# Order of the start, banks of the output weights, a second junk buffer and shuffled priorities in an attention-then-SoLU kernel

## The chip, the cores and the metric

The kernel runs on one core of a Trainium2 chip. The metric is device time in microseconds (us) of one execution. The engines are PE (TensorE), ACT (ScalarE), DVE (VectorE), POOL (GpSimd) and SP (SyncE, which issues nearly all DMAs); each takes its own instructions strictly in the order in which the program lists them, and waits on semaphores for the others.

## The reference

Two layers run one after the other. The first is attention over a set with 32 inducing points: per batch (4 batches of 12608 rows of 128 channels) `h = mab(inducing, x)` pools all rows into 32 vectors, and `mab(x, h)` lets every row attend to these 32. The second is a feed-forward layer of width 1024 on each of the 50432 rows:

```python
def mab(q, kv):
    s = scale * (q @ kv.transpose(0, 2, 1))
    s = s - s.max(-1, keepdims=True)
    a = np.exp(s)
    a /= a.sum(-1, keepdims=True) + 1e-09
    return a @ kv
h = mab(I, x); y = mab(x, h)              # 4 x 12608 x 128
h = y @ w_in                              # 128 -> 1024
e = np.exp(h - h.max(-1)); solu = h * e / (e.sum(-1) + 1e-09)
mu = solu.mean(-1); var = ((solu - mu) ** 2).mean(-1)
out = ((solu - mu) / np.sqrt(var + 1e-06) * g_ln) @ w_out    # 1024 -> 128
```

Attention inputs are 32-bit floats; the three weights of the second layer come as 64-bit floats and are rounded on the chip.

## The kernel before, in words

A tile is 128 rows of x; a batch has 99 tiles, the whole job 396. Four tiles make a group.

*Phase 1 of a batch* (`p1`) reads x, transposes it on PE, copies it out on ACT, stores the transposed x in DRAM, takes scores against the inducing points, a running maximum (DVE, with a small matmul that folds the four row groups), the exponentials (ACT), a transposition (DVE), and a weighted sum on PE. `combine` turns the sum into h and multiplies it by the input weights (`h4`, `hs`). Batch 0 runs this at the start of the kernel, in nine pieces of up to 12 tiles; the phase 1 of a later batch runs in between the tiles of the batch ahead.

*Phase 2 of a batch* (`p2`) computes each row's 32 attention weights, transposed (`aT`).

*The body* goes over the tiles. PE multiplies `aT` by `hs` (L1233, two matmuls of 512 columns, which use two of the four 32-row groups of the array); DVE scales and takes the row minimum (L1275); ACT takes the exponential and its sum (L1286); POOL multiplies (L1290); ACT squares the product for the variance (L1301), of which only the accumulated sum is used: the squares themselves go to a junk buffer `sq`; DVE transposes the product into `vt` (L1317). When four tiles of a group have come, PE multiplies them by the output weights `wc` in 32 steps of small matmuls (L1473), for each pair of row groups; these fill the row groups that L1233 leaves free. `evacuate` (L1501, DVE or ACT) and `finish` (L1526 to L1551) normalize and store.

*The weights.* `weights_in` and `weights_out` load and round the 64-bit weights (L434 to L454, on DVE, ACT and POOL). The output weights are then scaled by the gains (L492, ACT, eight instructions), their mean is taken (L501, PE) and subtracted (L506, DVE), and each quarter is spread to all four row groups (L544, PE; L522, copies by ACT or DVE) into `wc`.

*Memory for results of PE.* At the start the PSUM is cut into eight banks of 512 columns (`bank_e`, the locks `EARLY_TR` and `EARLY_PB`); `handover` gives it up for four buffers of 1024 (`h0` to `h3`, the lock `H`) that the body uses. The handover waits for phase 1 of batch 0, for `hs`, for the first `aT`, and for `wc`.

*What sets the order.* Each job is a generator that yields operations with a planned cost and a priority. The class `Planner` keeps a clock for each engine; among the operations of an engine that would be ready within a slack (`SLACK`) it takes the one with the lowest priority number, and writes its instruction. So the order on every engine is fixed when the program is built, from planned costs. A tile's priority number is its place t in the job; an offset for each kind of operation is added to it. PE's idle time is filled with transposes of the identity (L557), which do no work.

The function `beats` writes steps of PE: in each it emits one matmul for each of the two pairs of row groups that has work.

Of the kernel before, what the change touches and what calls it, by code (L numbers as in the profile page):

```python
# [10 lines left out]
BF16 = mybir.dt.bfloat16  # L11
# [8 lines left out]
P = 128  # L20
# [20 lines left out]
SLOTS = 3  # L41
PIECE = 4
TOKENS = 4
TURN_ON = 90
# [23 lines left out]
FILL = 400  # L68
FIRST = 4
LATE = -15  # L70
# [20 lines left out]
WOUT_X = -16.5  # L91
WOUT = -8
WIN = -18.5
# [22 lines left out]
class Op:  # L116
    def __init__(self, eng, cost, fn, *after, prio=None, alt=None, moves=0, late=0):
        self.eng, self.cost, self.fn, self.after, self.prio, self.alt, self.moves = eng, cost, fn, after, prio, alt, moves
        self.late = late
# [22 lines left out]
class Planner:  # L142
# [61 lines left out]
    def _pe(self, start, cost):  # L204

        at = start
        while True:
# [8 lines left out]
            self.busy[k] = self.busy.get(k, 0.0) + took  # L216
# [20 lines left out]
    def run(self):  # L237
        clock = self.clock
        while self.ops:
            first = min(self.ops, key=lambda o: (max(clock[o[0].eng], o[1]), o[3]))  # L240
            eng = first[0].eng
            limit = max(clock[eng], first[1]) + self.slack[eng]
            pick = min(
                (o for o in self.ops if o[0].eng == eng and o[1] <= limit),
                key=lambda o: (o[2][1] if o[0].prio is None else o[0].prio, o[3]),
# [8 lines left out]
            end = start + (self._pe(start, op.cost) if eng == "PE" else op.cost)  # L254
# [9 lines left out]
def set_attention_then_solu_kernel(ctx: ExitStack, tc: tile.TileContext, x, inducing, w_in, w_out, g_ln, out):  # L264
# [55 lines left out]
    sq = buf([P, FF], "sq", BF16)  # L320
# [14 lines left out]
    BULK = Lock([None] * TOKENS)  # L335
    ST = Lock([
# [84 lines left out]
    w_in_ready = Event()  # L421
# [54 lines left out]
    def weights_in():  # L476
        g = yield from rounded(w_in_sb, w_in.bitcast(U32), conv, None, conv_free, WIN)
# [5 lines left out]
    def weights_out():  # L483
# [12 lines left out]
        yield turned[NP[0] - 1]  # L496
        mp, rel = yield EARLY_PB.at(LATE)

# [4 lines left out]
        d = yield Op("PE", KC * 215, mean, d, rel, prio=LATE)  # L503
# [7 lines left out]
        give(EARLY_PB, mp, d)  # L511
# [7 lines left out]
        last, laid = [], [o]  # L519
# [4 lines left out]
        def laid_out(sp, q, k0, dp):  # L524
            dc = yield Op(
                "ACT", 570, out_of(nc.scalar.copy, sp, q, k0), dp, o, prio=LATE,
                alt=Op("DVE", 620, out_of(nc.vector.tensor_copy, sp, q, k0), dp, o, prio=LATE),
            )
            give(EARLY_PB, sp, dc)
# [4 lines left out]
        def spread(k0):  # L534
            four, free = [], []
            for q in range(4):
                sp, rel = yield EARLY_PB.at(LATE)
                four.append(sp)
                free += rel

            def copies():
                for q, sp in enumerate(four):
                    r = slice(q * M, (q + 1) * M)
                    nc.tensor.matmul(sp, lhsT=fold2[r, :], rhs=wg2[r, k0 * C : (k0 + half) * C], start=True, stop=True)  # L544

            dp = yield Op("PE", 1200, copies, d, free, prio=LATE)
            last.append(dp)
            if len(last) == 2:
                give(HN, wg2, *last)
            for q, sp in enumerate(four):  # L550
                spawn(laid_out(sp, q, k0, dp), LATE)

        for k0 in (0, half):
            spawn(spread(k0), LATE)
# [43 lines left out]
    def p1(b, k):  # L598
# [9 lines left out]
        halves = [(0, GS), (GS, n)] if early and not k and n > GS else [(0, n)]  # L608
        if not early:
            halves = [(c, min(c + PIECE, n)) for c in range(0, n, PIECE)]  # L610
        for c0, c1 in halves:
            for nbytes, fn in move(b, s0 + c0, c1 - c0, xn[:, c0:, :], False):
                trel = () if early else (yield BULK)[1]
                d = yield dma(nbytes, fn, rel, trel)
                if not early:
                    give(BULK, None, d)
# [1063 lines left out]
```

## Time and profile before

| what | value |
|---|---|
| time, median of 3 runs | 1184.61 us (1183.17 to 1184.68) |
| the profiled execution's own time | 1182.92 us |
| its span, first to last instruction | 1181.1 us |
| PE, busy | 1151.1 us, 97% |
| ACT, busy | 1102.6 us, 93% |
| DVE, busy | 1074.8 us, 91% |
| POOL, busy | 1065.6 us, 90% |
| tiles | 396 |

The profile is of one execution. The ends of matmuls are modelled, so that PE's 97% is not PE at its peak. An engine's idle time counts only what lies between its records; two records of one engine can overlap where one instruction's end runs beside the next one's start.

### The profile page before, as it was taken

What the parts mean: (1) busy time and instruction counts of PE and PEld (TensorE: products, weight loads), DVE (VectorE), ACT (ScalarE), POOL (GpSimd) and SP (SyncE); (2) the same over time, 40 slices, a digit from 0 to 9 for tenths busy, and PEclk for the clock granted to TensorE, in tenths of its full rate; (3) what the DMA queues carried; (4) which work ended last, traced back from release to release, by engine and by line L of the source; (5) the groups of instructions that cost most, each with busy time, mean ns of one, the idle gap of its engine ahead of it and who ended that gap; (6) DMA issues with size and microseconds to landing.
All of it is one profiled execution on the core that took longest, in us unless ns stands there. A gap on an engine that the chain in (4) does not pass through costs nothing.

```text
span 1181.1 us, 68196 instructions
## 1 busy us (share of the span) xinstructions
PE 1151.1 (97%) x30636; PEld 1055.0 (89%) x30636; DVE 1074.8 (91%) x1639; ACT 1102.6 (93%) x2191; POOL 1065.6 (90%) x612
## 2 busy tenths in 40 slices
PE   9999999999999999999999999999999999999996
PEld 7669989998889898999899999999988999999996
DVE  6799989898999899999899998999999999999981
ACT  5699899999999999999999999999999999999994
POOL 3399799898999989899899998989999999999994
PEclk9989999999999999999999999999999999999999
DMA  9532342522143433331423433341313131220103
GB/s 340 230 124 76 111 121 71 155 73 49 41 119 86 141 111 107 96 104 33 120 66 94 121 107 120 102 127 45 101 40 84 40 79 34 67 64 5 49 5 87
DMA packets 166884, 110.62 MB, mean 94 GB/s; under 512 B 78112, under 2 KB 131776, under 8 KB 166464
## 3 DMA queue, kind: packets, MB, share of 16 engines
q1 hardware_dynamic: 166592, 106.27, 31.0%
q8 instruction: 239, 3.92, 1.4%
q14 instruction: 53, 0.43, 0.1%
HBM read 53.51 MB, written 52.17 MB: 89 GB/s over the span
## 4 chain that ended last, share of the span: by engine, by line
PE 45%; POOL 23%; ACT 20%; issue 7%; DVE 3%; DMA 2%; SPq 0%; ACTq 0%; POOLq 0%; DVEq 0%
PE h L1473 32%; POOL eu L1290 16%; ACT sq L1301 9%; ACT eu L1286 6%; PE h L1233 4%; POOL spare L1290 3%; POOL spare L1547 3%; ACT spare L1286 1%; ACT xT L666 1%; ACT spare L1501 1%; PE h L850 1%; PE h L655 1%; ACT a L1013 1%; PE bank_e L557 1%; DMA dl<-dd 1%
## 5 line engine op out<-in xcount | busy, mean ns | idle before, releaser
L1473 PEld LDWEIGHTS h<-wc,vt 32*128 32x128 f32 (+1 forms) x25344 | 954.3, 185 | 45.8 <-issue 13.3
L1473 PE MATMUL h<-wc,vt 32*128 32x129 f32 (+1 forms) x25344 | 983.5, 273 | 10.4 <-ACT spare L1501 3.1
L1290 POOL TENSOR_TENSOR eu<-hn,eu 128x1024 f32<-128x1024 f32 x198 | 466.8, 2377 | 28.7 <-ACT eu L1286 27.7
L1233 PE MATMUL h<-hs,aT 32*128 32x512 f32 x1584 | 419.6, 607 | 6.0 <-DVE spare L1275 2.6
L1317 DVE STREAM_TRANSPOSE vt<-eu 128x1024 f32<-128x1024 f32 x327 | 397.7, 1229 | 11.4 <-POOL eu L1290 10.7
L1301 ACT ACTIVATE sq<-eu 128x1024 bf16<-128x1024 f32 x330 | 346.4, 1050 | 11.3 <-POOL eu L1290 6.5
L1290 POOL TENSOR_TENSOR eu<-spare,eu 128x1024 f32<-128x1024 f32 x132 | 311.7, 2379 | 11.2 <-ACT eu L1286 11.1
L1275 DVE TENSOR_SCALAR_CACHE_REDUCE hn<-h,rn 128x1024 f32<-128x1024 f32 x198 | 248.7, 1260 | 20.6 <-PE h L1233 12.2
L1275 DVE TENSOR_SCALAR_CACHE_REDUCE spare<-h,rn 128x1024 f32<-128x1024 f32 x198 | 248.2, 1260 | 20.7 <-PE h L1233 10.0
L1286 ACT ACTIVATE eu<-hn,nm 128x1024 f32<-128x1024 f32 x198 | 225.4, 1139 | 2.9 <-DVE hn L1275 2.7
L1290 POOL TENSOR_TENSOR spare<-spare 128x1024 f32<-128x1024 f32 x66 | 156.9, 2377 | 12.2 <-ACT spare L1286 12.2
L1286 ACT ACTIVATE eu<-spare,nm 128x1024 f32<-128x1024 f32 x132 | 150.4, 1140 | 2.3 <-DVE vt L1317 1.3
L1233 PEld LDWEIGHTS h<-hs,aT 32*128 32x128 f32 x1584 | 124.6, 186 | 27.5 <-DVE spare L1275 8.1
L1317 DVE STREAM_TRANSPOSE vt<-spare 128x1024 f32<-128x1024 f32 x65 | 80.0, 1231 | 2.0 <-POOL spare L1290 1.8
L1547 POOL TENSOR_TENSOR spare<-spare,fin 128x512 f32<-128x512 f32 x79 | 79.8, 1041 | 1.6
L1301 ACT ACTIVATE sq<-spare 128x1024 bf16<-128x1024 f32 x66 | 69.3, 1050 | 6.9 <-POOL spare L1290 5.3
L1286 ACT ACTIVATE spare<-spare,nm 128x1024 f32<-128x1024 f32 x66 | 75.2, 1140 | 0.4 <-DVE spare L1275 0.4
L1301 ACT ACTIVATION_READ_ACCUMULATOR sq<-eu 128x1 f32 x330 | 62.6, 190 | 0.0
L655 PE MATMUL h<-ident,xn 32*128 32x32 f32 x1188 | 53.6, 227 | 0.1
L655 PEld LDWEIGHTS h<-ident,xn 32*128 32x128 f32 x1188 | 51.1, 141 | 1.1 <-issue 0.8
L1501 ACT COPY spare<-h 128x774 f32<-128x774 f32 (+3 forms) x66 | 42.5, 646 | 9.3 <-PE h L1473 7.0
L666 ACT COPY xT<-h 128x1024 f32<-128x1024 f32 (+2 forms) x42 | 37.8, 900 | 1.1 <-PE h L655 1.1
(189 smaller groups left out, 849.6 us busy)
## 6 DMA issues: line engine op xcount, KB each, us to landing
out_dram<-spare SPq DMA_DIRECT2D x95, 256.0 KB, 3.3
xT<-xd SPq DMA_DIRECT2D x93, 256.0 KB, 3.8
xn<-in_x_dram SPq DMA_DIRECT2D x73, 256.0 KB, 3.7
xd<-xT SPq DMA_DIRECT2D x72, 256.0 KB, 2.6
dl<-dd SPq DMA_DIRECT2D x392, 1.0 KB, 2.3
xd<-vt SPq DMA_DIRECT2D x7, 768.0 KB, 10.2
spare<-in_x_dram SPq DMA_DIRECT2D x5, 768.0 KB, 9.3
dd<-qe SPq DMA_DIRECT2D x95, 4.0 KB, 2.1
```

The lines of the kernel that those rows point to most:

```text
L557: nc.tensor.transpose(out=bank[:, :P], in_=ident, identity=ident)
L655: nc.tensor.transpose(out=tr[:, k * 512 + s * M : k * 512 + (s + 1) * M], in_=xn[r, s, :], identity=ident[r, r])
L666: lambda: nc.scalar.copy(xT.rearrange("c s (q t) -> c q s t", q=4)[:, 2 * w : 2 * w + 2, :n, :], tr.rearrange("c (k x) -> c k x", k=2)[:, ...
L1233: nc.tensor.matmul(hp[:, cols], lhsT=aT[rows, i // 2, :], rhs=hs[rows, cols], start=True, stop=True)
L1275: lambda: nc.vector.tensor_scalar(out=hn, in0=hp, scalar1=rn, scalar2=None, op0=ALU.mult, op1=ALU.min, accum_out=nm),
L1286: "ACT", 1133, lambda: nc.scalar.activation(e, hn, AF.Exp, bias=nm, scale=-1.0, accum_out=G["qe"][:, s, 1:2]), d, rel, srel,
L1290: d = yield Op("POOL", 2330, lambda: nc.gpsimd.tensor_tensor(out=e, in0=hn, in1=e, op=ALU.mult), de, prio=t + PR_MU)
L1301: "ACT", 1040, lambda: nc.scalar.activation(sq, e, AF.Square, scale=1.0 / 32.0, accum_out=G["qe"][:, s, 0:1]), d,
L1317: lambda: nc.vector.transpose(out=G["vtb"][:, : n * FF].rearrange("p (j s t) -> p j s t", j=M, s=n)[:, :, s, :], in_=e.rearrange("p (a f) ...
L1473: nc.tensor.matmul(op[:rows, a - 2 * w, :], lhsT=vt[q, k, :], rhs=wc[q, k, :], start=(k == 0), stop=(k == JB - 1))
L1501: return lambda: eng(to, at)
L1547: return lambda: eng.tensor_tensor(out=raw, in0=raw, in1=y[:, i0 : i0 + 4].unsqueeze(2).to_broadcast([rows, 4, C]), op=ALU.mult)
```

## The change

1. *Start.* The x of batch 0 is loaded in pieces of four tiles throughout (before: up to twelve), 26 transfers where there were 12, each piece of x after the one before; the output weights are loaded later, behind the fifth of the nine pieces.
2. *Output weights.* The handover no longer waits for `wc`. The mean, the subtraction and the spread come after it and use buffers of `H`. The products wait for `wc` by an event.
3. *First tiles.* Until the first products are opened (`flow["quiet"]`) two tiles' first matmuls are issued in one step (`mm1_two`), alternating between the pairs of row groups and writing two buffers of `H`; and the transposes of `aT` and x are done whole (128 rows) and not by 32 rows.
4. *Junk.* Two buffers `sq0` and `sq1` are used in turn.
5. *Planner.* In each stretch of 20 us of planned time a pair from the table `JS` (a width and a turn) adds a pseudo-random offset, up to half the width either way, to the priorities: 41 of its 60 entries have a width above 0, from 1.5 to 25. Some constants change; a tile's first matmul is chosen among four tiles, before among three.

```diff
+STRETCH = 20
+JS = [
+    (4, 317), (4, 297), (10, 664), (1.5, 67), (1.5, 612), (0, 0), (4, 454), (25, 293),
...
-FILL = 400
+FILL = 200
-LATE = -15
+LATE = -22
-SLACK = {"PE": 0, "ACT": 400, "DVE": 100, "POOL": 100, "SP": 0}
+SLACK = {"PE": 100, "ACT": 400, "DVE": 100, "POOL": 100, "SP": 0}
-WINDOW_TILES = 3
+WINDOW_TILES = 4
...
+            stretch = int(limit / 1000 / STRETCH)
+            wide, turn = JS[stretch] if stretch < len(JS) else (0, 0)
             pick = min(
                 (o for o in self.ops if o[0].eng == eng and o[1] <= limit),
-                key=lambda o: (o[2][1] if o[0].prio is None else o[0].prio, o[3]),
+                key=lambda o: ((o[2][1] if o[0].prio is None else o[0].prio) + wide * ((o[3] * 40503 + turn * 7919) % 1009 / 1009 - 0.5), o[3]),
             )
...
-    sq = buf([P, FF], "sq", BF16)
+    sq_b = bufs(2, [P, FF], "sq", BF16)
+    squares = [0]
...
     def weights_out():
+        yield loaded[WOUT_AT]
...
+        if MEAN_H:
+            yield handed
+            where = H
+        else:
+            yield turned[NP[0] - 1]
+            where = EARLY_PB
+        mp, rel = yield where.at(LATE)
...
+        yield handed
...
         for k0 in (0, half):
-            spawn(spread(k0), LATE)
+            for w in range(2):
+                hb, rel = yield H.at(WC_PR)
+                op = Op("PE", 950, None, d, rel, prio=WC_PR)
...
-        halves = [(0, GS), (GS, n)] if early and not k and n > GS else [(0, n)]
-        if not early:
-            halves = [(c, min(c + PIECE, n)) for c in range(0, n, PIECE)]
+        halves = [(c, min(c + PIECE, n)) for c in range(0, n, PIECE)]
+        if early and k:
+            yield loaded[k - 1]
...
+                    if flow["quiet"] and len(left) > 1:
+                        two = [(s, part_of[b, ff_groups[j][0] + s]) for s in left[:2]]
...
+                        yield TURN
+                        hp2, hrel2 = yield H.at(t + H_LAST)
+
+                        def mm1_two():
+                            hs = hT[b][1]
+
+                            for k in range(2):
+                                for (s, (ka, i)), hb in zip(two, (hp, hp2)):
+                                    r = i % 2 * 2
+                                    rows = slice((r + k) * M, (r + k + 1) * M)
+                                    cols = slice(k * 512, (k + 1) * 512)
+                                    aT = aT_of[(b, ka)]["aT"][0]
+                                    nc.tensor.matmul(hb[:, cols], lhsT=aT[rows, i // 2, :], rhs=hs[rows, cols], start=True, stop=True)
...
+            def squared():
+                squares[0] += 1
+                nc.scalar.activation(sq_b[squares[0] % 2], e, AF.Square, scale=1.0 / 32.0, accum_out=G["qe"][:, s, 0:1])
+
+            ds = yield Op("ACT", SQ_NS, squared, d, prio=t + PR_SQ)
...
+        yield wc_ready
+        flow["quiet"] = False
...
-        for e in (early_turned, wc_ready):
+        for e in (early_turned,) if MEAN_H else (early_turned, centred):
...
+        plan.set(handed, *done)
```

The order on DVE at the end of phase 1 of batch 0. L454 (after: L477) is the last step of rounding the output weights, L506 (L536) the subtraction of their mean, L760 and L792 (L797 and L829) the maxima, L844 (L881) the transposition of exponentials, L919 (L956) the copy of `h4`, L1001 (L1038) the first transposition of phase 2. Before:

```order
L882 SCALAR_TENSOR_TENSOR acc_125<-acc_125,small_120,bank_e_77 128x128
L454 SCALAR_TENSOR_TENSOR hn_82<-aT_96,hn_82 128x1024
L882 SCALAR_TENSOR_TENSOR acc_125<-acc_125,small_121,bank_e_78 128x128
L792 TENSOR_SCALAR small_122,m_123<-bank_e_79,m_123 128x4
L760 TENSOR_REDUCE small_119<-bank_e_74 64x1
...
L844 STREAM_TRANSPOSE spare<-spare 128x256
L506 TENSOR_TENSOR hn_82<-bank_e_75,hn_82 128x1024
L882 SCALAR_TENSOR_TENSOR acc_125<-acc_125,small_122,bank_e_79 128x128
L833 TENSOR_SCALAR l_124<-l_124,small_119 128x1
L843 MEMSET eT 64x32
L844 STREAM_TRANSPOSE ew<-eT 128x224
L522 COPY wc<-bank_e_76 128x4x128
```

And after:

```order
L881 STREAM_TRANSPOSE spare<-spare 128x256
L880 MEMSET eT 64x32
L870 TENSOR_SCALAR l_125<-l_125,small_120 128x1
L881 STREAM_TRANSPOSE ew<-eT 128x224
L919 SCALAR_TENSOR_TENSOR acc_126<-acc_126,small_123,bank_e_79 128x128
L949 TENSOR_SCALAR small_121<-bank_e_73 128x1
L950 RECIPROCAL small_121<-small_121 128x1
L919 SCALAR_TENSOR_TENSOR acc_126<-acc_126,small_120,bank_e_75 128x128
L956 COPY h_0_118<-bank_e_73 128x128
L477 SCALAR_TENSOR_TENSOR hn_82<-aT_97,hn_82 128x1024
L1038 STREAM_TRANSPOSE s_0_88<-bank_e_76 128x128
```

The three steps of the output weights that stood among the maxima and transpositions have moved: the last rounding step to behind the copy of `h4`, the subtraction and the copies to behind the first tiles.

The order on PE from the first tile on, before (L1233 is a tile's first matmuls, L991 the scores of phase 2, L1057 the transposes of `aT` by 32 rows):

```order
L991 MATMUL h_730<-vt,h_0_117 32x256 x4
L1233 MATMUL h_732<-hs,aT_94 128x512 x2
L1233 MATMUL h_733<-hs,aT_94 128x512 x2
L1233 MATMUL h_730<-hs,aT_94 128x512 x2
L991 MATMUL h_731<-xT_86,h_0_117 32x512 x4
L1233 MATMUL h_732<-hs,aT_94 128x512 x2
L1057 MATMUL h_733<-ident,a_93 128x32 x8
L1057 MATMUL h_730<-ident,a_93 128x32 x8
```

And after (L1278 is the step of two tiles, L531 the mean, L579 the spread, L1063 the whole transposes of `aT`):

```order
L1278 MATMUL h_693<-hs,aT_95 128x512
L1278 MATMUL h_691<-hs,aT_95 128x512
L1278 MATMUL h_693<-hs,aT_95 128x512
L1278 MATMUL h_691<-hs,aT_95 128x512
L531 MATMUL h_694<-hn_82,ones_mean 128x128 x8
L1028 MATMUL h_692<-xT_87,h_0_118 32x512 x4
L1063 MATMUL h_691<-ident,a_94 128x128 x4
L579 MATMUL h_693<-hn_82,fold 128x512 x2
L579 MATMUL h_694<-hn_82,fold 128x512 x2
L579 MATMUL h_691<-hn_82,fold 128x512 x2
L1278 MATMUL h_693<-hs,aT_97 128x512
L1278 MATMUL h_694<-hs,aT_97 128x512
```

Tiles come two at a time, and the mean and the spread stand between the second and the third pair, in the same buffers as the tiles.

The order on ACT in the body, with waits, before (`sq` is the junk buffer; Activation is ACT's own semaphore):

```order
L1286 ACTIVATE eu_84,qe2_104<-hn0_80,nm3_115 128x1024 [waits DVE_49]
L1301 ACTIVATE sq_83,qe2_104<-eu_84 128x1024 [waits Activation_49,Pool_49]
L1301 ACTIVATE sq_83,qe2_104<-spare_66 128x1024 [waits Activation_49,Pool_49]
L1301 ACTIVATE sq_83,qe2_104<-eu_84 128x1024 [waits Activation_49,Pool_49]
L1286 ACTIVATE eu_84,qe3_106<-hn2_82,nm0_112 128x1024 [waits DMAHW3_49,DVE_49]
```

And after, at such a place:

```order
L1362 ACTIVATE eu_85,qe0_101<-hn1_81,nm2_115 128x1024 [waits DVE_49]
L1378 ACTIVATE sq0_83,qe0_101<-eu_85 128x1024 [waits Activation_49,Pool_49]
L1378 ACTIVATE sq1_84,qe3_107<-eu_85 128x1024 [waits Activation_49]
L1362 ACTIVATE spare_66,qe0_101<-spare_66,nm3_116 128x1024 [waits DVE_49]
L1378 ACTIVATE sq0_83,qe0_101<-eu_85 128x1024 [waits Activation_49,Pool_49]
L1378 ACTIVATE sq1_84,qe0_101<-eu_85 128x1024 [waits Activation_49,Pool_49]
L1608 ACTIVATE fin0_110<-dl0_109,tiny_131 128x20 [waits DMAHW2_49,DMAHW3_49,DMAHW1_49,DMAHW0_49]
```

Before, a square waits for the end of the square that last wrote `sq`: in 70 of 396 places that is the instruction just ahead. After, squares follow each other directly in 84 places, and the value that such a square waits for on ACT's semaphore is never that of the instruction just ahead (the nearest is two back); of other instructions, six exponentials and 18 of the copies of `evacuate` now wait for the instruction just ahead, before none and 8.

## Rows read from the trace of the kernel before

**Rows 1.** The page: the span, and the engines' busy time.

```profile
span 1181.1 us, 68196 instructions
PE 1151.1 (97%) x30636; PEld 1055.0 (89%) x30636; DVE 1074.8 (91%) x1639; ACT 1102.6 (93%) x2191; POOL 1065.6 (90%) x612
```

**Rows 2.** Windows, busy us of PE, PEld, DVE, ACT, POOL in each stretch.

```profile
60.00:80.00 20.00, 18.07 (x210) 9.98 (x210) 20.00 (x31) 19.68 (x37) 17.35 (x10) 0.83 0.38 121
100.00:900.00 800.00, 790.24 (x21982) 733.27 (x21981) 748.05 (x1124) 771.70 (x1518) 742.78 (x420) 1.00 0.33 94
900.00:1150.00 250.00, 245.18 (x6878) 232.14 (x6874) 239.45 (x317) 241.62 (x478) 249.69 (x138) 0.99 0.20 46
```

**Rows 3.** The page: the chain that ended last, by engine.

```profile
PE 45%; POOL 23%; ACT 20%; issue 7%; DVE 3%; DMA 2%; SPq 0%; ACTq 0%; POOLq 0%; DVEq 0%
```

**Rows 4.** The timeline from 37 to 55 us: start, length, engine, line, idle before.

```profile
37.50 1.22 DVE L454 SCALAR_TENSOR_TENSOR hn<-aT,hn 128x1024 f32<-128x1024 int32 x1
...
38.75 2.45 ACT L492 ACTIVATE hn<-hn,g_sb 128x128 f32<-128x128 f32 x8 [2.00 <-DVE hn L454]
...
41.28 0.15 DVE L799 TENSOR_SCALAR small<-m 128x1 f32<-128x1 f32 x1
...
41.73 0.28 ACT L822 ACTIVATE small<-m,small 128x1 f32<-128x1 f32 x1
...
42.78 0.19 ACT L824 ACTIVATION_READ_ACCUMULATOR eT<-bank_e,small 64x1 f32 x1
...
42.91 1.23 DVE L506 TENSOR_TENSOR hn<-bank_e,hn 128x1024 f32<-128x1024 f32 x1 [0.60 <-PE bank_e L501]
...
44.74 0.41 DVE L844 STREAM_TRANSPOSE ew<-eT 128x224 f32<-128x224 f32 x1
...
45.58 0.64 PE L850 MATMUL bank_e<-xn,ew 128*32 128x128 f32 x14
45.67 1.29 DVE L522 COPY wc<-bank_e 128x512 f32<-128x512 f32 x2 [0.52 <-PE bank_e L544]
45.71 1.08 ACT L522 COPY wc<-bank_e 128x512 f32<-128x512 f32 x2 [2.75 <-PE bank_e L544]
...
48.73 0.28 DVE L919 COPY h<-bank_e 128x128 f32<-128x128 f32 x1
...
49.95 0.32 DVE L1001 STREAM_TRANSPOSE s<-bank_e 128x128 f32<-128x128 f32 x1 [0.35 <-PE bank_e L991]
...
52.87 1.99 PE L1233 MATMUL h<-hs,aT 32*128 32x512 f32 x12
```

**Rows 5.** Waits: who waited for whom, us in total, times, longest.

```profile
POOL eu L1290 <- ACT eu L1286: 38.8, 38, 2.7
DVE hn L1275 <- PE h L1233: 12.2, 18, 1.5
```

**Rows 6.** The timeline of ACT from 313 us: exponentials and squares.

```profile
313.95 0.19 ACT L1301 ACTIVATION_READ_ACCUMULATOR sq<-eu 128x1 f32 x1
314.05 1.14 ACT L1286 ACTIVATE eu<-hn,nm 128x1024 f32<-128x1024 f32 x1
...
316.12 0.19 ACT L1301 ACTIVATION_READ_ACCUMULATOR sq<-eu 128x1 f32 x1
316.41 1.06 ACT L1301 ACTIVATE sq<-spare 128x1024 bf16<-128x1024 f32 x1
```

**Rows 7.** Windows at the start; the last two columns are DMA share and GB/s.

```profile
0.00:10.00 10.00, 8.64 (x52) 8.43 (x53) 1.42 (x9) 2.62 (x4) 0.70 (x6) 1.00 0.82 269
10.00:28.00 18.00, 17.73 (x214) 12.81 (x213) 15.61 (x41) 11.65 (x27) 8.55 (x6) 1.00 1.07 374
```

**Rows 8.** The page: DMA issues, KB each, us to landing.

```profile
xn<-in_x_dram SPq DMA_DIRECT2D x73, 256.0 KB, 3.7
```

More of the change, by code (lines that the diff above doesn't have):

```diff
@@ L41 @@
 SLOTS = 3
+STRETCH = 20
+SQ_NS = 1049
+JS = [
[8 rows of a table added]
+]
 PIECE = 4
 TOKENS = 4
+ETOK = 8
+WIN_AT = 1
+WOUT_AT = 4
+MEAN_H = 1
+PAIRED = 1
+HALF = 0.5
+WC_PR = -15
 TURN_ON = 90
@@ L202, in _step, with _pe @@
                 value = want.free.pop(0)
-    def _pe(self, start, cost):
+    def _pe(self, start, cost, weight=1.0):
         at = start
@@ L215, in _pe @@
             took = min(room, cost * rate)
-            self.busy[k] = self.busy.get(k, 0.0) + took
+            self.busy[k] = self.busy.get(k, 0.0) + took * weight
             at += took
@@ L253, in run @@
             op.fn()
-            end = start + (self._pe(start, op.cost) if eng == "PE" else op.cost)
+            end = start + (self._pe(start, op.cost, op.weight) if eng == "PE" else op.cost)
             clock[eng] = end
@@ L510, in weights_out @@
         )
-        give(EARLY_PB, mp, d)
+        give(where, mp, d)
+        plan.set(centred, d)
         freed = []
@@ L532, in laid_out, with copies @@
                 plan.set(wc_ready, *laid)
[L534 to L551, printed above, removed]
-        for k0 in (0, half):
-            spawn(spread(k0), LATE)
+        parts = []
+        for k0 in (0, half):
+            for w in range(2):
+                hb, rel = yield H.at(WC_PR)
+                op = Op("PE", 950, None, d, rel, prio=WC_PR)
+                def copies():
+                    for i in range(2):
+                        q = 2 * w + i
+                        r = slice(q * M, (q + 1) * M)
+                        nc.tensor.matmul(
+                            hb[:, i * 512 : (i + 1) * 512], lhsT=fold2[r, :], rhs=wg2[r, k0 * C : (k0 + half) * C], start=True, stop=True
+                        )
+                op.fn = copies
+                dp = yield op
+                parts.append(dp)
+                both = []
+                for i in range(2):
+                    spawn(laid_out(hb, i, 2 * w + i, k0, dp, both), WC_PR)
+        give(HN, wg2, *parts)
     def fill(bank):
@@ L675, in by_rows @@
                 plan.set(copied, *ready)
-        if not early:
+        rows_only = not early and not flow["quiet"]
+        if rows_only:
             ways = [0, 1]
@@ L680, in p1 @@
                 spawn(by_rows(ways), PRIO_P1(b, k))
-        for c0 in range(0, n if early else 0, most):
+        for c0 in range(0, 0 if rows_only else n, most):
             c1 = min(c0 + most, n)
@@ L1088, in p2 @@
         turned_too = Event()
-        if early:
-            assert n % 2 == 0 and pairs <= 4
+        whole_turn = early or flow["quiet"] and n % 2 == 0
+        if whole_turn:
+            assert n % 2 == 0 and pairs <= (4 if early else 8)
             spawn(turned_whole(), PRIO_P2(b, j))
-        for _ in range(0 if early else 2):
+        for _ in range(0 if whole_turn else 2):
             spawn(turned_rows(), PRIO_P2(b, j))
@@ L1131, in set_attention_then_solu_kernel @@
                 js = js[len(same) :]
+    turn_of = {bj: i for i, bj in enumerate((b, j) for b in range(NB) for j in order[b])}
+    began = [[Event() for _ in turn_of] for _ in range(2)]
     stream = [[], []]
-    flow = {"idle": Event(), "left": 2 * NB * NG - 2, "half": False, "took": 0}
+    flow = {"idle": Event(), "left": 2 * NB * NG - 2, "half": False, "took": 0, "quiet": bool(PAIRED)}
     def going(w, at):
@@ L1162, in beats @@
             full = went + bool(also) > 1
+            beat += 1 if full else HALF
+            flow["weight"] = beat / (i + 1)
             flow["took"] += BEAT + (TURN_ON if full and flow["half"] else 0)
@@ L1484, in products @@
         stream[w].append(dict(j=0, emit=emit, ready=ready, close=close, prio=t + PR_G2))
+        plan.set(began[w][turn_of[b, j]])
         if not last:
@@ L1613, in handover @@
         late = pool("late", 1, PSUM, side="right")
-        for i in range(4):
-            give(H, buf([P, FF], f"h{i}", where=late), *done)
+        banks = [buf([P, FF], f"h{i}", where=late) for i in range(4)]
+        for hb in banks:
+            give(H, hb, *done)
         plan.scratch = (H,)
+        plan.set(handed, *done)
         for k in range(NP[0]):
```

70 lines of the change are left out of this document (45 added, 25 removed), and 7 rows, old and new, of the table JS.

## The prediction

> **What bounds the kernel now.** The page's first section shows four engines between 90 and 97% busy [rows 1], which alone names no bound. The windows split it [rows 2]. From 100 to 900 us ACT is busy 771.7 of 800 us (96.5%), DVE 748.1 and POOL 742.8; from 900 to 1150 us, where no phase 1 of a later batch is left, POOL is busy 249.7 of 250. PE's busy figure can't be set beside these, since the ends of its matmuls are modelled; that PE is needed is seen in the chain of waits: 45% of the chain lies on PE, 23% on POOL, 20% on ACT [rows 3]. So up to 900 us several engines bind by turns, ACT the fullest, and behind that POOL alone. The start is a chain of short steps in which every engine has room: its first tile begins at 52.87 us [rows 4], 4.5% of the span with no output. I read the timeline of the start for what stands between the last maximum and that tile, and ACT's timeline for what stands between two squares [rows 6].
>
> **The change part by part.** The sum is against the profiled execution, 1182.9 us (span 1181.1 and 1.8 around it), 1.7 under the median of 1184.6.
>
> *Start, what goes.* Three steps of the output weights leave the chain. (a) L454, 1.22 us on DVE from 37.50, stood ahead of the last two maxima; DVE had been fed without a break to them: −1.2. (b) The gains, 2.45 us on ACT from 38.75, and the eighth piece's exponentials that they held back, delayed those of the ninth: its maximum was done at 41.43 (41.28 + 0.15), its factor started at 41.73 (L822): −0.3. (c) L506, 1.23 us from 42.91, began just as the last exponentials ended (42.97 = 42.78 + 0.19) and pushed the last transposition to 44.74: −1.2. The matmul L850 that follows it started at 45.58, 0.43 us after the transposition's end at 45.15, behind the spread; some 0.1 is PE's usual delay: −0.3. Together −3.0. What comes in its way: L454's counterpart now stands between the copy of `h4` (ends 49.01) and the score transposition (49.95), a hole of 0.94 us for 1.2 us of work: +0.3. First tile at about 50.2, net −2.7 [all rows 4].
>
> *Start, what comes back.* The mean, the subtraction and the spread are not saved but done behind the first tiles, where DVE is busy 20.00 of 20 us and ACT 19.68 [rows 2]. DVE takes the subtraction (1.23) and three copies of 0.65 (1.29 for two), 3.2 us; ACT five copies of 0.54 (1.08 for two), 2.7 us [rows 4]. On DVE the gain of 2.7 is thus paid back with 3.2 by about 80 us, while POOL, 17.35 of 20 there and the bound at the end, keeps its lead if it is fed. PE's granted clock there, a mean of 0.83 of 2.4 GHz, does not enter, as DVE and not PE is full.
> The pairs of first matmuls have no row of before. They need two free buffers of four, so DVE can run dry while PE waits for the second. Bounds: DVE waited for L1233 18 times for 12.2 us, 0.7 us each [rows 5]; five pairs behind the first, 0 to 3.4 us. The start as a whole so lies between −2.7 and +4 (3.2 − 2.7 + 3.4). I take −1, near the end that POOL's row speaks for, as POOL alone binds later.
>
> *Loading.* The x comes in 26 transfers for 12. A transfer of 256 KB lands 3.7 us after its issue [rows 8]; with eight out at a time (nine issues on, each waits for the one eight before) that allows 2 MB in 3.7 us, 570 GB/s, more than the 374 that were reached between 10 and 28 us [rows 7]: 0.
>
> *Junk buffers.* An exponential behind a square starts while the square's accumulator is read: the reading starts at 313.95 and lasts to 314.14, the next instruction starts at 314.05. A square behind a square starts at 316.41, 0.10 after the reading's end (316.12 + 0.19) [rows 6]. Offset from the reading's start: 0.10 against 0.29, so the wait for `sq` costs 0.19 us each time; 70 times, 13.3 us of ACT. The 16 new waits of other instructions for the one just ahead take back 3.0, priced alike: 10.3. The Trainium skill (ScalarE: Activation LUTs, "What ACT_TABLE_LOAD costs") says that back-to-back ACTIVATEs overlap by about 93 ns. The trace agrees for the exponential (0.09), and by that figure alone the 54 net waits would be worth 5.0 us.
> What reaches the end: 56 of the 70 pairs come before 900 us, among squares 1 to 296; behind that POOL is full and ACT's time is worth nothing. That leaves 8.2 us (0.8 of 10.3). Ends: −8.2 if ACT bound all of that stretch, −1.6 by ACT's 20% of the chain [rows 3], 0 if none. ACT's 96.5% is the fullest figure there, so I go beyond the chain's share: −4.
>
> *Order.* The shuffled priorities move instructions of all engines over 41 stretches, and the counts of work hardly change. No row shows what a given order is worth. Bound: POOL waited 38.8 us for exponentials at L1290, over 38 waits [rows 5]. A third of it either way, 13 us, is what an order better or worse could give. On PE the choice among four tiles gives `beats` one more chance to fill both pairs of row groups, which is not less than before. Value −1, ends ±13.
>
> Sum: −1 − 4 − 1 = −6: 1176.9 by the profiled execution, 1178.6 by the median. I say 1178.
>
> **The rivals.**
> *R1, nothing arrives* (1183): the start's gain is spent on DVE by 80 us, and ACT's freed time turns into waits for PE or POOL. For it: 45% of the chain on PE, whose matmuls stay the same 12672 products and 792 first matmuls; DVE at 20.00 of 20. Against: ACT at 96.5% up to 900 us, in which waits for exponentials hold POOL. Sum: start 0 (2.7 − 3.2 rounded), junk −1.6 by the chain's share, order 0: 1183.
> *R2, slower* (1190): a shuffled order is fixed by planned costs; an operation put up to 12.5 tiles behind its rank (width 25, half either way) holds everything behind it on its engine. Place: the queues of ACT and DVE ahead of POOL, in the 41 stretches. Price: one wait of POOL for an exponential is 1.0 us (38.8 / 38). With one more of it on the path in a third of the stretches, 14 us come in, and with −5 from the other two terms 1193; with one in a quarter 1190. From six such waits on it eats the forecast's gain. Against: only nine stretches have the full width, and the slack lets few operations compete.
> *R3, the pieces load slower* (1185): if 256-KB transfers moved only the 269 GB/s of the first 10 us instead of 374 [rows 7], the 6.7 MB of 10 to 28 us would take 25 us, and the first tile comes 7 us later: 1185. The Trainium skill (DMA: Bandwidth & Descriptors, "Measured (HBM→SBUF, 128 partitions, SWDGE, issued from GpSimd)") asks for 1 MiB or more per DMA and lists 341 GB/s at 1 MB and 138 at 64 KB, which speaks against this split; an estimate between the two, 240 GB/s, would give some 10 us. Against it, by the trace: the eight transfers that are out together.
> *R4, more* (1166): the order takes a third of POOL's waits away besides (−13).
>
> **How the numbers follow.** A measurement of this kernel tells a change from none at about 0.2%, 2.4 us: faster is below 1182.2, slower above 1187.0. Forecast (1173 to 1183, by most of the start's and the junk buffers' ends) 0.52, R1 0.17, R2 0.12, R3 0.06, R4 0.13. Faster: 0.50 of the forecast, 0.06 of R1, all of R4, 0.01 of R3: 0.70. Slower: all of R2, 0.02 of R3, 0.01 of R1: 0.15. Within: 0.15. For 8 in 10 I leave out half of R2 and the far part of R4: 1166 to 1189.
>
> **What would show it.** In the profile after: the first matmul of a tile near 50 us, with no weight step among the last maxima (start); DVE still full for the 20 us behind it and first products no earlier than before; a square directly behind a square starting 0.10 us after the reading's start (junk), ACT's time per tile down and its idle time not up by as much; x landing by 28 us as before (R3). The forecast is wrong if POOL's waits for exponentials grow (R2) or halve (R4), if ACT's freed time shows as ACT waiting for POOL (R1), or if DVE waits over 3 us for the paired matmuls.

## The result and the profile after

The kernel after takes 1172.36 us (median of 4 runs, 1171.71 to 1172.71), the kernel before, run beside it, 1184.64 (1183.17 to 1186.55). The ratio is 0.9895, 95% interval 0.9878 to 0.9912: 12.3 us faster. The forecast was 1178, range 1166 to 1189. The direction and the range held; the size was twice what was summed up, and the lines and runs below show which terms of the sum were off.

The page after, its span, the busy time of the engines and the chain of waits by engine (the lines that answer to [rows 1, 3]):

```profile
span 1170.9 us, 67965 instructions
PE 1140.9 (97%) x30531; PEld 1048.1 (90%) x30531; DVE 1071.8 (92%) x1634; ACT 1102.5 (94%) x2192; POOL 1063.0 (91%) x614
...
PE 48%; POOL 22%; ACT 14%; DVE 7%; issue 6%; DMA 2%; SPq 1%; ACTq 0%; POOLq 0%; DVEq 0%
```

ACT, DVE and POOL are as busy as before to within 3 us, so the 10.2 us by which the span is shorter are, on these three, idle time that went. ACT's share of the chain fell from 20% to 14%, DVE's rose from 3% to 7%. Where the idle time went is seen in the windows after (columns as in [rows 2, 7]):

```profile
10.00:28.00 18.00, 16.79 (x202) 11.39 (x201) 15.23 (x43) 12.69 (x29) 6.73 (x7) 1.00 1.07 371
60.00:80.00 20.00, 17.62 (x175) 11.16 (x176) 20.00 (x36) 19.90 (x36) 16.76 (x9) 0.88 0.36 122
100.00:900.00 800.00, 792.22 (x22198) 739.22 (x22194) 756.98 (x1138) 777.97 (x1536) 749.29 (x423) 1.00 0.33 95
900.00:1140.00 240.00, 234.21 (x6614) 220.32 (x6610) 228.05 (x302) 233.22 (x459) 239.24 (x133) 1.00 0.18 42
```

Between 100 and 900 us POOL is busy 6.5 us more than before (749.29 against 742.78), DVE 8.9 and ACT 6.3 more: in the same time more was done. From 900 us on POOL was full already and is so still, and nothing can be won there. Between 10 and 28 us, while x is loaded, 371 GB/s were moved where it was 374.

A finer measure is the time at which POOL starts its k-th product (L1290, after L1366), from the span's start. For before in us, for the others the difference to it (minus is earlier); the last column is the span. The other kernels are those of the experiments below:

| kernel | product 0 | 20 | 120 | 300 | 395 | span |
|---|---|---|---|---|---|---|
| before | 56.7 | 110.3 | 398.1 | 909.6 | 1159.6 | 1181.1 |
| after | −6.0 | +1.1 | −10.1 | −9.2 | −8.8 | −10.2 |
| before_two | −0.5 | +4.4 | +3.5 | +0.3 | +0.1 | −0.1 |
| after_one | −5.8 | +3.0 | −6.9 | −4.4 | +0.6 | +0.1 |
| after_plain | −1.4 | +3.8 | +3.4 | +6.7 | +6.7 | +14.0 |
| after_prefix3 | −5.3 | −1.3 | +3.2 | +6.0 | +6.2 | +15.3 |
| after_prefix20 | −4.9 | +2.6 | −8.5 | −1.1 | +1.9 | +7.8 |
| after_turn1 | −0.6 | +5.8 | +10.7 | +19.2 | +21.8 | +29.0 |
| before_sw399 | −0.5 | +6.7 | +6.4 | +9.1 | +9.7 | +19.1 |
| sw399_tail | −0.4 | +5.1 | +4.8 | +9.8 | +9.7 | +10.6 |

These are single profiled executions; the verdicts below go by the medians. The granted clock of PE was 0.994 in that of before and 0.996 in that of after, but between 0.982 and 0.991 in the others, so a part of their later columns is the clock (last section). The kernel after begins 6.0 us earlier, has lost all of that by product 20, leads by 10.1 us at 400 us, keeps most of that, and wins another 1.4 behind the last product.

The start after, some lines of the timeline:

```profile
37.85 0.15 DVE L836 TENSOR_SCALAR small<-m 128x1 f32<-128x1 f32 x1
...
39.87 0.40 DVE L881 STREAM_TRANSPOSE ew<-eT 128x224 f32<-128x224 f32 x1
...
42.77 0.29 DVE L956 COPY h<-bank_e 128x128 f32<-128x128 f32 x1 [1.10 <-PE bank_e L954]
42.98 1.22 DVE L477 SCALAR_TENSOR_TENSOR hn<-aT,hn 128x1024 f32<-128x1024 int32 x1
44.11 0.31 DVE L1038 STREAM_TRANSPOSE s<-bank_e 128x128 f32<-128x128 f32 x1
...
46.83 1.14 PE L1278 MATMUL h<-hs,aT 32*128 32x512 f32 x8 [0.52 <-ACT aT L1068]
...
51.00 2.02 PE L531 MATMUL h<-hn,ones_mean 128*128 128x128 f32 x16
...
53.50 1.22 DVE L536 TENSOR_TENSOR hn<-h,hn 128x1024 f32<-128x1024 f32 x1
```

Against [rows 4], the last maximum is done 3.4 us earlier (38.00 for 41.43), the last transposition of exponentials 4.9 (40.27 for 45.15), the copy of `h4` 6.0 (43.06 for 49.01) and the first tile 6.0 (46.83 for 52.87). The mean (L531) and its subtraction (L536) stand behind the first two pairs of tiles.

Two squares after, on ACT, and who waited for whom (us in total, times, longest):

```profile
125.17 1.05 ACT L1378 ACTIVATE sq<-eu 128x1024 bf16<-128x1024 f32 x1
126.11 0.19 ACT L1378 ACTIVATION_READ_ACCUMULATOR sq<-eu 128x1 f32 x1
126.21 1.04 ACT L1378 ACTIVATE sq<-spare 128x1024 bf16<-128x1024 f32 x1
```

```profile
POOL eu L1366 <- ACT eu L1362: 50.9, 40, 5.4
DVE hn L1351 <- PE h L1278: 4.3, 2, 2.8
POOL spare L1366 <- ACT spare L1362: 6.0, 7, 1.4
```

The line of before that answers to the last of these, and that [rows 5] leave out:

```profile
POOL spare L1290 <- ACT spare L1286: 12.2, 9, 4.3
```

The second square starts 0.10 us after the reader's start (126.21 − 126.11), where it was 0.29 in [rows 6]. POOL's waits for exponentials in the buffer `eu` grew from 38.8 [rows 5] to 50.9, those in `spare` fell from 12.2 to 6.0; together they grew from 51.0 to 56.9, in a kernel that is faster. That total did not tell the direction.

### The profile page after: what moved, and what is told of

The parts are those of the page before. It is cut to its first block, busy times and chain, and to the rows that moved or that the text cites. A ratio compares the mean times of both kernels' runs of the same rounds, so it can differ in the third digit from the quotient of the medians.

```text
span 1170.9 us, 67965 instructions
## 1 busy us (share of the span) xinstructions
PE 1140.9 (97%) x30531; PEld 1048.1 (90%) x30531; DVE 1071.8 (92%) x1634; ACT 1102.5 (94%) x2192; POOL 1063.0 (91%) x614
## 4 chain that ended last, share of the span: by engine, by line
PE 48%; POOL 22%; ACT 14%; DVE 7%; issue 6%; DMA 2%; SPq 1%; ACTq 0%; POOLq 0%; DVEq 0%
PE h L1554 37%; POOL eu L1366 16%; ACT sq L1378 5%; PE h L1308 4%; ACT eu L1362 4%; POOL spare L1366 3%; DVE vt L1394 2%; POOL spare L1629 2%; DVE hn L1351 2%; DVE spare L1351 2%; DMA spare<-in_x_dram 1%; ACT spare L1583 1%; PE h L690 1%; PE h L1095 1%; PE h L1028 1%
## 5 line engine op out<-in xcount | busy, mean ns | idle before, releaser
L1554 PEld LDWEIGHTS h<-wc,vt 32*128 32x128 f32 (+1 forms) x25344 | 952.4, 185 | 39.2 <-issue 18.0
L1554 PE MATMUL h<-wc,vt 32*128 32x129 f32 (+1 forms) x25344 | 979.0, 273 | 7.1 <-ACT spare L1583 2.2
L1366 POOL TENSOR_TENSOR eu<-spare,eu 128x1024 f32<-128x1024 f32 x173 | 409.6, 2378 | 26.0 <-ACT eu L1362 25.9
L1308 PE MATMUL h<-hs,aT 32*128 32x512 f32 x1528 | 405.7, 601 | 6.1 <-DVE hn L1351 1.8
L1366 POOL TENSOR_TENSOR eu<-hn,eu 128x1024 f32<-128x1024 f32 x157 | 372.4, 2380 | 25.3 <-ACT eu L1362 25.0
L1351 DVE TENSOR_SCALAR_CACHE_REDUCE spare<-h,rn 128x1024 f32<-128x1024 f32 x200 | 250.8, 1259 | 17.2 <-PE h L1308 9.1
L1362 ACT ACTIVATE eu<-spare,nm 128x1024 f32<-128x1024 f32 x173 | 197.2, 1140 | 1.0 <-DVE spare L1351 0.6
L1362 ACT ACTIVATE eu<-hn,nm 128x1024 f32<-128x1024 f32 x157 | 179.0, 1140 | 4.4 <-DVE hn L1351 3.9
L1366 POOL TENSOR_TENSOR spare<-hn,spare 128x1024 f32<-128x1024 f32 x39 | 92.7, 2378 | 4.7 <-ACT spare L1362 4.7
L1366 POOL TENSOR_TENSOR spare<-spare 128x1024 f32<-128x1024 f32 x27 | 64.4, 2385 | 1.3 <-ACT spare L1362 1.3
L1362 ACT ACTIVATE spare<-hn,nm 128x1024 f32<-128x1024 f32 x39 | 44.4, 1139 | 0.0
```

Of the source, the lines that this page charges most:

```text
L1308: nc.tensor.matmul(hp[:, cols], lhsT=aT[rows, i // 2, :], rhs=hs[rows, cols], start=True, stop=True)
L1351: lambda: nc.vector.tensor_scalar(out=hn, in0=hp, scalar1=rn, scalar2=None, op0=ALU.mult, op1=ALU.min, accum_out=nm),
L1362: "ACT", 1133, lambda: nc.scalar.activation(e, hn, AF.Exp, bias=nm, scale=-1.0, accum_out=G["qe"][:, s, 1:2]), d, rel, srel,
L1366: d = yield Op("POOL", 2330, lambda: nc.gpsimd.tensor_tensor(out=e, in0=hn, in1=e, op=ALU.mult), de, prio=t + PR_MU)
L1554: nc.tensor.matmul(op[:rows, a - 2 * w, :], lhsT=vt[q, k, :], rhs=wc[q, k, :], start=(k == 0), stop=(k == JB - 1))
```

## The experiments

Two theories stood at first. One: a wait on ACT lies on the path, and the two junk buffers take it away. The other: the order that the table chose is what pays. All kernels of a comparison ran on one chip beside the kernel before.

**The junk buffers on the kernel before (before_two).** Only this is changed; the order of every engine stays.

```diff
-    sq = buf([P, FF], "sq", BF16)
+    sq_b = bufs(2, [P, FF], "sq", BF16)
...
-                nc.scalar.activation(sq, e, AF.Square, ...)
+                nc.scalar.activation(sq_b[squares[0] % 2], e, AF.Square, ...)
```

> The kernel before with two junk buffers in turn and nothing else; the order of every engine is unchanged, and 70 waits of a square for the square just ahead are gone (13.3 us of ACT at 0.19 us each). Theory W (the wait of ACT is on the path): 1184.6 - 4 to 8 = about 1177 to 1181. Rival O (the order is what pays; ACT's freed time turns into other waits): 1183 to 1185.

Measured: 1182.25 us, ratio 0.9965 (0.9951 to 0.9980), by the ratio 4.1 us less (2.4 to 5.8). From one reader's start to the next square's the median is 93 ns in 70 places, as in the kernel after.

**One junk buffer on the kernel after (after_one).**

```diff
-                nc.scalar.activation(sq_b[squares[0] % 2], e, AF.Square, ...)
+                nc.scalar.activation(sq_b[0], e, AF.Square, ...)
```

> The changed kernel with one junk buffer, order unchanged: 84 squares wait again for the square just ahead (16.0 us of ACT). Theory W: slower than the changed kernel by 5 to 9 us, 1177 to 1181. Rival O: 1172 to 1174.

Measured: 1178.87 us, ratio 0.9944 (0.9925 to 0.9964); the kernel after, which ran at another time, is at 0.9895, so one buffer costs about 5.8 us by the two ratios. Its chain, and two squares of it:

```profile
PE 41%; ACT 27%; POOL 12%; issue 8%; DVE 6%; DMA 3%; SPq 2%; ACTq 0%; DVEq 0%; POOLq 0%
```

```profile
96.68 0.18 ACT L1378 ACTIVATION_READ_ACCUMULATOR sq<-spare 128x1 f32 x1
96.96 1.06 ACT L1378 ACTIVATE sq<-eu 128x1024 bf16<-128x1024 f32 x1
97.92 0.18 ACT L1378 ACTIVATION_READ_ACCUMULATOR sq<-eu 128x1 f32 x1
98.20 1.06 ACT L1378 ACTIVATE sq<-eu 128x1024 bf16<-128x1024 f32 x1
```

The square starts 0.28 us behind the reader's start; over 84 places the median is 278 ns, against 93 with two. With one buffer ACT's share of the chain is 27%, with two 14%. The wait, its 0.19 us and its place on the path are shown in both directions; of the 5.8 us a part can be the clock, as said further down.

**No shuffle (after_plain), and another shuffle (after_turn1).** In the first all widths of the table are taken as 0, in the second each entry of the table turns the pseudo-random numbers one step further. All else is the kernel after.

```diff
-            wide, turn = JS[stretch] if stretch < len(JS) else (0, 0)
+            wide, turn = 0, 0
```

```diff
             wide, turn = JS[stretch] if stretch < len(JS) else (0, 0)
+            turn += 1
```

> The changed kernel with all widths of JS at 0: new start, two junk buffers, no shuffled priorities. Theory W with the start (start -4, wait -5, table worth nothing): 1173 to 1177. Rival O (the table is worth as much as the rest): 1178 to 1184.

> The changed kernel with every turn of JS raised by one: same widths, another pseudo-random order. If any shuffle of these widths is as good as another: 1171 to 1175, as the changed kernel. If the table's own turns matter (rival O): slower than the kernel without shuffling, 1180 to 1190.

Measured: 1196.75 us without a shuffle, ratio 1.0099 (1.0083 to 1.0116), and 1211.43 with another, ratio 1.0221 (1.0203 to 1.0239). One more run of the kernel without a shuffle, on another chip (plain_tail), took 1195.97. The table is worth 24 us against none, and 39 against the one other table that was run. The expectation that the table is worth nothing fell, and so did the one that any shuffle of these widths is as good. Without the table the kernel is 12 us slower than before, although it has the new start and the two buffers; how much of this the start, and how much the changed constants of the planner (`FILL`, `LATE`, `SLACK`, `WINDOW_TILES`) bring, no run separates.

**An order changed by next to nothing (before_sw399).** On the kernel before.

```diff
-SWITCH = 400
+SWITCH = 399
```

> Kernel before with one planned cost changed: a change of PE from the body's work to other work is planned at 399 ns and not 400. Nothing else is written otherwise; the orders of the engines part from some early place on. Theory L (the order of the whole program is a draw, its value is carried to the chip, and the clock that the planner keeps while the kernel is built shows it): that clock ends at 1194.4 us here and at 1181.7 for the kernel before, so the time is 12.7 us over before, some 1197. Rival N (such differences exist in the plan alone, the chip evens them out): as before, within 3 us.

Measured: 1200.78 us, ratio 1.0144 (1.0120 to 1.0169), 17 us slower. A nanosecond in one planned cost moves the time more than the whole change does. So the time of an order is to a large part a draw, and beside this one the kernel before was a good draw.

**A part of the table (after_prefix3, after_prefix20).** The first 3 or 20 entries stay, the rest is (0, 0).

> Kernel after with the first three entries of the table (60 us of planned time) and no shuffle behind them. Theory L: the start is that of the kernel after (first tile at 46.8 us, 4.6 us ahead of the kernel without any shuffle is how the planner's table bought it if it is the table that did), but what follows is a new draw; the planner's clock ends at 1200.5, so about 1201, slower than the kernel without any shuffle (1196.8) in spite of the earlier start. Rival S (what the start gains is kept to the end): first tile at 46.8 and the end as much earlier than without any shuffle, 1196.8 - 8.5 = 1188.

> Kernel after with the first 20 entries of the table (400 us) and no shuffle behind them. Theory L: tiles begin at the times of the kernel after up to about 400 us and fall behind from there; the planner's clock ends at 1189.4, so 1191 to 1193, 20 us over the kernel after. Rival F (the table pays at the start and in the first stretches, where POOL is not full, and the rest is ballast): the lead of 1 us at 400 us over the kernel before is kept, and the two junk buffers bring their 4 us: 1175 to 1180.

Measured: 1197.35 us, ratio 1.0114 (1.0091 to 1.0137), and 1190.06, ratio 1.0046 (1.0027 to 1.0065). With three entries the first product comes 3.9 us earlier than without any (−5.3 against −1.4 in the table above), and the time is the same: an earlier start alone brings nothing. With 20 entries the lead at product 120 is 8.5 us, nearly the kernel after's, and nearly gone by product 300 (1.1). So the table's gain is not made once at the start; the entries behind the 20th bring a large part of it.

**Order alone on the kernel before (before_js).** The same shuffle with a table of its own; 11 of its 60 entries have a width above 0 (not 13, as the expectation has it).

> Kernel before with the shuffle of the planner and a table of its own, found by trying some 1400 entries one stretch after the other and keeping what made the planner's clock end earlier (13 of 60 stretches are shuffled); one junk buffer and the start as before. Theory L: the planner's clock ends at 1178.2 against 1181.7, so the time is 3.5 us less, ratio 0.997. Rival N: the plan is better on paper alone: ratio 1.000 or above. It also bounds what order alone brings without the two other parts of the change: the junk buffers alone brought 4.1.

Measured: 1185.15 us, ratio 1.0008 (0.9990 to 1.0026): no gain. The planner's clock promised 3.5 us. But the 12 runs had a mean granted clock of 0.986, and the 20 of before beside them 0.9905; by the line of the last section that is an estimated 3.4 us, so that this pair does not decide whether a difference of 3.5 us in the plan is carried over. Large ones are: over before_sw399, after_plain, after_turn1 and the two prefixes the planner's clock at the end of the build (1194.4, 1197.0, 1213.4, 1200.5 and 1189.4) and the measured median differ by 0.2 to 6.4 us, while the medians span 21; in before_js they differ by 7.0. The same clock ends at 1181.7 for the kernel before and at 1168.5 for the kernel after: building the two shows 13.2 us of difference, where 12.3 were measured. It knows nothing of the wait for the junk buffer, as before_two and after_one end at the same figures as before and after.

**The last 30 us (after_tail, sw399_tail, plain_tail2).** The spans in the table above grow by more than the last product does: from that product's end to the end of the last computing instruction the kernel before takes 14.4 us, after 13.2, but before_sw399 22.4, after_plain 20.5 and after_turn1 20.4. (The rest of the span, 4.6 to 6.2 us in these, is the last store.) PE at the end of before_sw399 (L1473 products of earlier groups, L1395 those of the last group's own tiles), and POOL's last instructions:

```profile
1172.96 5.34 PE L1473 MATMUL h<-wc,vt 32*96 32x129 f32 x180 [0.42 <-ACT spare L1501]
1178.23 1.09 PE L1371 MATMUL h<-ident,eu 128*128 128x128 f32 x8
1179.16 1.04 PE L1371 MATMUL h<-ident,spare 128*128 128x128 f32 x8
1180.79 3.84 PE L1395 MATMUL h<-xn,vt 128*128 128x129 f32 x32 [0.60 <-ACT vt L1380]
1184.56 2.25 PE L1473 MATMUL h<-wc,vt 32*96 32x129 f32 x72
```

```profile
1188.47 0.22 POOL L1528 TENSOR_TENSOR fin<-dl,fin 128x16 f32<-128x16 f32 x1 [16.82 <-ACT fin L1527]
...
1190.97 3.04 POOL L1547 TENSOR_TENSOR spare<-spare,fin 128x512 f32<-128x512 f32 x3
```

And PE at the end of the kernel after (L1554 and L1472 are the same two):

```profile
1147.51 0.92 PE L1554 MATMUL h<-wc,vt 32*96 32x129 f32 x24
1148.36 2.05 PE L1472 MATMUL h<-xn,vt 128*128 128x129 f32 x16
1150.34 6.68 PE L1554 MATMUL h<-wc,vt 32*96 32x129 f32 x232
1156.95 1.97 PE L1448 MATMUL h<-ident,eu 128*128 128x128 f32 x16
1159.51 3.84 PE L1472 MATMUL h<-xn,vt 128*128 128x129 f32 x32 [0.60 <-ACT vt L1457]
```

A matmul of 32-bit floats has two records here (25344 for the 12672 products), so x72 are 36 products. In before_sw399 these 36, of an earlier group, stand behind everything else, and their evacuation, the finish and POOL's three multiplications follow one after the other, after POOL has idled 16.82 us. In the kernel after the last of the earlier groups' products are done at 1157.02, and the finish runs beside the last group's work, after POOL has idled 4.74 us:

```profile
1157.94 0.23 POOL L1610 TENSOR_TENSOR fin<-dl,fin 128x16 f32<-128x16 f32 x1 [4.74 <-ACT fin L1609]
```

The edit puts the last group's own products behind the others:

```diff
-        d = yield Op("PE", SWITCH + 225 * KC, add, got, rel, wrel, prio=t - 55)
+        d = yield Op("PE", SWITCH + 225 * KC, add, got, rel, wrel, prio=t + 60)
```

> Kernel after with one priority changed: the last group's own output products (L1472, one batch of 8 matmuls for each of its four tiles) get the priority t + 60 instead of t - 55, so that on PE they stand behind the products of the groups before (L1554). Nothing else moves. Theory E (part of what an order is worth lies in the last 30 us, in which of the two stands first on PE): in the kernel after, the products of the groups before end 6.3 us ahead of the last L1472 already, but 16 of the 32 L1472 stand ahead of part of them; 1 to 2 us less, about 1171, ratio 0.988. Rival B (the last 30 us wait for POOL's last product, whatever stands on PE): 1172.4, no change.

> The kernel before with the planned cost of 399 ns, and its last group's output products behind those of the groups before, as in the other kernel of this kind. Theory E: in its trace 72 products of an earlier group stand behind the last of them, and the evacuation, the finish and POOL's last three multiplications run after everything else; moved, the time falls by 7 to 9 us from 1200.8 to about 1192.5, and what stays over the kernel before (8 us) is the order in the body. Rival B: 1200.8, since the work is the same and only its order on PE changes.

> The kernel after without the shuffle (1196.8), and its last group's output products (L1472) behind those of the groups before (L1554), as in the two other kernels of this kind. Theory E: in its trace 148 products stand behind the last L1472, and 20.5 us pass from POOL's last product to the end, 7.3 more than in the kernel after; moved, some 7 of the 24 us between the two go: 1189 to 1190, and the rest, some 17 us, is the order of the body. Rival B: 1196.8.

Measured: sw399_tail 1193.32 us, ratio 1.0065 (1.0043 to 1.0087), against 1.0144 without the edit; plain_tail2 1190.00, ratio 1.0040 (1.0020 to 1.0061), against 1.0099. PE at the end of sw399_tail:

```profile
1168.14 7.41 PE L1473 MATMUL h<-wc,vt 32*96 32x129 f32 x256
1175.48 2.05 PE L1395 MATMUL h<-xn,vt 128*128 128x129 f32 x16
1177.37 1.04 PE L1371 MATMUL h<-ident,eu 128*128 128x128 f32 x8
1178.24 1.04 PE L1371 MATMUL h<-ident,spare 128*128 128x128 f32 x8
1179.11 3.96 PE L1395 MATMUL h<-xn,vt 128*128 128x129 f32 x32
```

So about 7 of the table's 24 us are a single place, which of two groups of matmuls stands first on PE at the end; the other 17 came before the last product (the column of product 395: +6.7 without the table, −8.8 with it) and are the order of the start and the body. after_tail, where that place was right already but for 16 of the last group's 32 matmuls, measured 1170.77 us, ratio 0.9877 (0.9855 to 0.9899). Its median is the lowest of this study, but its interval overlaps that of the kernel after (0.9878 to 0.9912): by the medians the 1 to 2 us expected are not told apart from none. In its profile the stretch from the last product's end to the end of the span is 14.4 us, in that of the kernel after 17.7, which speaks for theory E there too.

## Why the prediction was right or wrong

*Start, what goes.* Right in place, too small: 6.0 us for 2.7. The steps named did leave the chain, but the last maximum came 3.4 us earlier, where (a) and (b) had 1.5; the last transposes of x came at 31.10 instead of 32.39, which the sum had at 0. (PE's usual delay behind DVE, 0.1 in the sum, is 0.05 in the trace of before, which moves nothing.) Much of this is the table's doing: in after_plain the first product starts 1.4 us earlier and not 6.0, since without the table the last rounding step L477 stands ahead of the copy of `h4` again and the mean ahead of the first tile:

```profile
42.57 1.19 DVE L477 SCALAR_TENSOR_TENSOR hn<-aT,hn 128x1024 f32<-128x1024 int32 x1
...
45.17 0.29 DVE L956 COPY h<-bank_e 128x128 f32<-128x128 f32 x1 [1.02 <-PE bank_e L954]
...
49.13 2.05 PE L531 MATMUL h<-hn,ones_mean 128*128 128x128 f32 x16
51.11 1.14 PE L1278 MATMUL h<-hs,aT 32*128 32x512 f32 x8
```

*Start, what comes back.* Right: the lead is gone by product 20 (+1.1), and DVE is full from 60 to 80 us. DVE waited for the paired matmuls 4.3 us in two waits, over the 3 us that were to show the forecast wrong. after_prefix3 shows that a start 3.9 us earlier brings nothing by itself, so −1 was about right for the net.

*PE's clock at the start.* The sentence that it "does not enter, as DVE and not PE is full" was wrong; the section on the hardware has the rows.

*Loading.* Right: 371 GB/s, and R3 did not come. The last x landed at 28.9 us instead of 27.8, and its last transposes came earlier all the same.

*Junk buffers.* Right in mechanism and in the price of one wait, 0.19 us. The size, −4 forecast, came out at −4.1 on the kernel before and −5.8 on the kernel after, where 84 and not 70 squares stand behind a square; but −4 was a choice between −1.6 and −8.2, and that it came so near is in part luck. The nine runs of after_one had a mean granted clock of 0.9927, the four of the kernel after 0.9955; by the line of the last section an estimated 2.1 of the 5.8 us go with that. That nothing is won behind 900 us fits before_two (its lead does not change from product 300 to 395). In after_one's profiled execution 5.0 us are lost there all the same: its granted clock fell to 0.96 between 1020 and 1160 us, and POOL, which is full there otherwise, idled 4.1 of these 140 us.

*Order.* This term was the furthest off: "Value −1, ends ±13". after_one holds the new start, constants and order without the second buffer, and its ratio of 0.9944 is 6.6 us; with the start at about nothing, some −6 where −1 was put. Its clock was higher than that of before beside it (0.9927 for 0.9895), an estimated 2.4 us of these, so the order itself gave some −4. The body shows that size at a granted clock of 1.00; after_one and then before_two:

```profile
100.00:900.00 800.00, 792.05 (x22106) 737.32 (x22102) 754.94 (x1136) 778.97 (x1531) 746.72 (x421) 1.00 0.34 95
100.00:900.00 800.00, 792.58 (x22074) 735.71 (x22072) 751.83 (x1129) 772.84 (x1526) 746.38 (x421) 1.00 0.33 94
```

Beside the 742.78 us of before, POOL got 3.9 us more done with the new order alone, 3.6 more with the second buffer alone, and 6.5 more with both. The sum's bound had no hold on this: it was drawn from POOL's waits for exponentials in one buffer, but over both buffers those grew by 5.9 us while the time fell, and the kernels with no table and with another table lie 24 and 39 us over the kernel after, more than the 13 us that an order better or worse was to give. "No row shows what a given order is worth" is true of the trace; the planner's clock, 13.2 us apart for the two kernels, would have shown it.

*The sign that misled.* "The forecast is wrong if POOL's waits for exponentials grow (R2)": they grew, and the time fell by twice the forecast.

*Rivals.* R1 fell: ACT did more in the same time. That an order can cost as much as R2 says is shown by after_turn1 (ratio 1.0221), but the table at hand is not an arbitrary one, and the prediction had no row that could tell the two apart; R2's mechanism is not shown, as POOL's waits for exponentials were 57.2 us in after_turn1, 6 more than before, where 26 us were lost. R4's 1166 was about as far from the measured time as the forecast, and its mechanism did not come, as POOL's waits grew.

## What to carry to other kernels

Where a program fixes the order on every engine from planned costs, the order is a term of its own, here as large as 2%, and a neutral edit draws it anew: compare two versions of such a kernel with the order held (as the two junk-buffer kernels do), or with several draws of each, and read what the planner's own clock says of the two before forecasting. Look at the last groups first, since there one misplaced block has nothing to hide behind. And when successive instructions of one engine write a result that nobody reads, give them two places to write it.

## What the runs showed of the hardware

The time of one and the same kernel went with its mean granted clock. Over 61 runs of the kernel before the clock lay between 0.984 and 0.995 and the time between 1190.3 and 1180.5 us; a straight line through them gives 0.75 us for each 0.001 (correlation −0.88). In before_two's profile most of the loss lies soon after the first tiles. Four windows from 55 to 95 us, of before and then of before_two, whose engines have the same instructions in the same order but for the second junk buffer:

```profile
55.00:65.00 10.00, 7.78 (x56) 2.34 (x48) 10.00 (x20) 9.38 (x18) 8.30 (x5) 1.00 0.67 210
65.00:75.00 10.00, 9.67 (x120) 5.78 (x120) 10.00 (x14) 9.82 (x17) 7.70 (x4) 0.68 0.02 4
75.00:85.00 10.00, 9.15 (x233) 8.15 (x229) 9.87 (x22) 10.00 (x22) 9.65 (x5) 0.98 0.67 212
85.00:95.00 10.00, 10.00 (x305) 9.41 (x300) 9.59 (x13) 9.82 (x19) 9.33 (x5) 1.00 0.38 110
```

```profile
55.00:65.00 10.00, 8.53 (x48) 3.14 (x48) 9.89 (x18) 9.48 (x18) 8.78 (x5) 0.71 0.66 211
65.00:75.00 10.00, 10.00 (x120) 6.01 (x112) 8.18 (x13) 7.99 (x16) 7.23 (x4) 0.50 0.01 2
75.00:85.00 10.00, 9.16 (x86) 6.55 (x86) 8.36 (x17) 9.19 (x19) 8.32 (x4) 0.50 0.64 210
85.00:95.00 10.00, 10.00 (x295) 10.00 (x290) 7.82 (x12) 7.26 (x14) 5.91 (x4) 0.92 0.32 82
```

From 55 to 60 us PE was busy 3.53 of 5 us in both; then one was granted 1.00 up to 65 us, and the other fell to 0.50 (the lower level, 1.2 GHz) and stayed there to 85 us. What decided it these rows do not show. At 0.50 DVE, full or nearly so in before, falls to 8.18 and 8.36 of 10 us, and before_two loses 4.9 us to before between products 0 and 20.

The four runs of the kernel after lay at 0.995 and 0.996, those of after_tail at 0.994 to 0.997. By the line above, 0.0059 more clock than before's mean of 0.9896 is an estimated 4.4 of the 12.3 us, a term that the prediction put at nothing. Whether the new start keeps the clock or the runs were lucky is open: after_one, which starts the same way, had 0.986 to 0.999 in nine runs. The clock does not make the other differences of order: before_sw399 ran at a mean of 0.985 and after_turn1 at 0.984, an estimated 3 to 4 of the 17 and 26 us that they lost, and after_plain, 12 us slower than before, at 0.9895.
